# Three sums of each up product: from VectorE and POOL to accumulating transfers between SBUF tiles

## The chip, the cores and the metric

One core of a Trainium2 chip runs the kernel. Its engines work side by side and each takes its own instructions in order: TensorE (PE in the profile) multiplies matrices into PSUM, VectorE (DVE) and ScalarE (ACT) read PSUM and SBUF, GpSimd (POOL) reads SBUF, SyncE (SP) here only begins transfers, and 16 DMA engines carry them out. An engine waits for another, or for a transfer, by semaphores. The metric is the device time of one execution in microseconds.

## The reference

Two blocks follow one another. The first is a linear attention without softmax, on 8 batches, 8 heads, 576 positions and 64 features, with an RMS norm. Its output, as 4608 rows of 512, goes through four experts; each row adds up the four results by its own weights.

```python
kv = einsum('bhsd,bhse->bhde', k, v)
out = einsum('bhsd,bhde->bhse', q, kv)
x = out / sqrt(mean(out * out, -1) + 1e-6) * g_norm      # then (b, s, h*d): 4608 x 512
p = domain_probs / (domain_probs.sum(-1) + 1e-9)
for e in range(4):
    h = maximum(x @ w1[e], 0)                            # "up": 512 -> 1024
    y += p[:, e:e+1] * (h @ w2[e])                       # "down": 1024 -> 512
```

All of it is float32, and the experts' products are nearly all of the work.

## The kernel before

The rows are cut into 9 blocks of 512, so there are 36 steps `s = e * 9 + c` (expert `e`, block `c`). In each step an up product and, one step behind, a down product run interleaved on TensorE. Each product is done by a seven-product scheme of Strassen's kind, in two levels: 7 outer products `m`, each made of 7 inner products `mm`. The blocks of the result are sums and differences of the outer products. It is these outer sums that the change is about.

The program does not give its instructions in the order in which they run. Every operation goes into a plan with a key (where in the steps it belongs), a cost on each engine that may take it, and its buffers. The plan then plays the program through by these costs and fixes for each engine which operation it takes and when, and in which buffer each value lies. That order is the one the chip runs.

```python
def layout(self, slots, later, idle, idle_banks, idle_until):
    ...                                   # (cut: choice of the operation with the nearest due time)
    if eng == "SP":
        ...
    else:
        op.end = busy[eng] = t + op.cost[eng]
        if op.kb:                         # a transfer begun on an engine other than SP
            op.end += 5.5
    if op.port:
        port = op.end                     # one "combine" at a time on VectorE or POOL
```

Costs of an operation on `n` elements a partition, and the helper that all elementwise sums in SBUF go through (line 360 of the profile):

```python
def dve(n):    return {"DVE": 0.155 + 0.00104 * n}
def act(n):    return {"ACT": 0.155 + 0.00088 * n}
def either(n): return {"DVE": 0.155 + 0.00104 * n, "POOL": 0.15 + 0.00225 * n}

def combine(key, cost, out_, a, b, op, reads, writes):
    plan.add(key, cost,
        lambda eng: adder(eng).tensor_tensor(out=out_(), in0=a(), in1=b(), op=op),
        reads=reads, writes=writes, port=True)
```

The up product of a step. Each outer product `m` is collected in a tile `made[m]` of 128 x 1024 (kind `big`, 29 tiles and later 4 more). ScalarE copies (line 900) and VectorE sums (line 908) bring it out of PSUM, and both free the PSUM bank for TensorE:

```python
OUTER = (1, 2, 6, 5, 3, 7, 4)
def up(s, e, views):
    made, h = {}, {}

    def add(key, to, a, b, op=ALU.add, where=either):
        combine(key, where(2 * NT), lambda: to.ap[:], lambda: a.ap[:], lambda: b.ap[:], op, [a, b], [to])

    def relu(key, b):                     # line 864, ScalarE, 128 x 1024
        ...

    for i, m in enumerate(OUTER):
        whole = made[m] = Buf("big", f"m{n}")
        ...                               # (cut: 7 inner products on TensorE, L881, with their copies and sums)
        key = s + (i + 1) / 7

        def unit(f):
            h[f] = Buf("big", f"h{f}_{s}")
            return h[f]

        if m == 2:
            add(key, unit(1), made[1], made[2])
            relu(key, h[1])
        elif m == 6:
            add(key, made[1], made[1], made[6])
        elif m == 5:
            add(key, made[6], made[1], made[5])
        elif m == 3:
            add(key, unit(21), made[6], made[3])
            relu(key, h[21])
            add(key, unit(7), h[1], h[21], ALU.subtract)
        elif m == 7:
            add(key, made[1], made[1], made[7])
            add(key, unit(4), made[1], made[5], where=dve)
            relu(key, h[4])
            ...                           # (cut: two more sums on VectorE)
        elif m == 4:
            add(key, unit(2), made[1], made[4])
            relu(key, h[2])
            add(key, unit(3), h[2], h[6], ALU.subtract)
```

The down product of the later experts begins its four groups with 0.2 of a step's offset, `h[1]` and `h[6]` first and `h[2]` in the third. Its results are added to the output in HBM by transfers begun on POOL (line 1065), 256 KB each:

```python
def send(key, i):
    ...
    nc.gpsimd.dma_start(out=dst, in_=cell(i)[parts, :], accum_op=ALU.add)   # e > 0; else a plain one on SP
```

Steps 9 to 35 have the inner scheme in the down product too (line 1170 on TensorE); the first expert's down product (line 1095) has one level, with matmuls of 256 columns. The forms of x for each step come from HBM by transfers begun on SP, one 512 KB form or two halves for each `m`.

Of the kernel before, what the change touches and what calls it, by code (L numbers as in the profile page):

```python
# [10 lines left out]
ALU = mybir.AluOpType  # L11
# [219 lines left out]
def kernel(  # L231
# [36 lines left out]
    nc = tc.nc  # L268
# [65 lines left out]
    plan = Plan()  # L334

    def pe(products, columns, passes=2):
        return {"PE": passes * products * (0.008 + 0.0008125 * columns) + 0.003}

    def dve(n):
        return {"DVE": 0.155 + 0.00104 * n}  # L340

    def act(n):
        return {"ACT": 0.155 + 0.00088 * n}
# [12 lines left out]
    def combine(key, cost, out_, a, b, op, reads, writes):  # L356

        plan.add(
            key, cost,
            lambda eng: adder(eng).tensor_tensor(out=out_(), in0=a(), in1=b(), op=op),  # L360
            reads=reads, writes=writes, port=True,
        )
# [485 lines left out]
    def block(b, a, t):  # L848
        return b.ap[:, (2 * a + t) * HN:(2 * a + t + 1) * HN]

    def up(s, e, views):
        made = {}
        h = {}

        def add(key, to, a, b, op=ALU.add, where=either):
            combine(
                key, where(2 * NT), lambda: to.ap[:], lambda: a.ap[:], lambda: b.ap[:], op,
                [a, b], [to],
            )

        def relu(key, b):
            plan.add(
                key, act(2 * NT),
                lambda eng: nc.scalar.activation(out=b.ap[:], in_=b.ap[:], func=ACT.Relu),  # L864
                reads=[b], writes=[b],
            )

        for i, m in enumerate(OUTER):
            n = f"{s}_{m}"
            whole = made[m] = Buf("big", f"m{n}")  # L870
            bank = {
                1: Buf("u1", f"u1_{n}"), 2: Buf("u2", f"u2_{n}"), 5: Buf("u2", f"u3_{n}"),
            }
            snap = {}
            for j, mm in enumerate(ORDER):
                key = s + (i + j / 7) / 7
                ps = bank[{2: 2, 5: 5, 3: 5}.get(mm, 1)]

                def product(eng, m=m, mm=mm, ps=ps):
                    for u in range(2):  # L880
                        nc.tensor.matmul(  # L881
                            ps.ap[:, u * P:(u + 1) * P],
                            lhsT=w1f[e][m][mm][1]()[:, u * P:(u + 1) * P], rhs=views[m][mm][1](),
                            start=(mm in (1, 5) and u == 0), stop=True, skip_group_check=True,
                        )

                op = plan.add(
                    key, pe(2, P), product,
                    reads=w1f[e][m][mm][0] + [views[m][mm][0]] + ([ps] if mm == 2 else []),
                    **{"parts" if mm == 2 else "writes": [ps]},  # L890
                    after=last[-2:-1] if mm == 1 else seeds if mm == 5 else (),
                )
                op.marks, op.seed = (ps, HN), mm == 2
                if mm == 3:
                    last.append(op)

                def copy(to, where, ps=ps, key=key):
                    return plan.add(
                        key - 0.4, act(HN),
                        lambda eng: nc.scalar.activation(  # L900
                            out=where(), in_=ps.ap[:, 0:HN], func=ACT.Copy),
                        reads=[ps], parts=[to],
                    )

                def total(a, t, src, add_, whole=whole, key=key):
                    plan.add(
                        key - 0.4, dve(HN),
                        lambda eng: nc.vector.tensor_tensor(  # L908
                            out=block(whole, a, t), in0=src.ap[:, 0:HN], in1=add_.ap[:], op=ALU.add),
                        reads=[src, add_], parts=[whole],  # L910
                    )

                if mm == 1:
                    seeds = [copy(bank[2], lambda b=bank[2]: b.ap[:, 0:HN])]
                elif mm in (6, 7):
                    snap[mm] = Buf("snap", f"s{mm}_{n}")
                    copy(snap[mm], lambda b=snap[mm]: b.ap[:])
                if mm == 2:
                    copy(whole, lambda whole=whole: block(whole, 0, 0))
                elif mm == 7:  # L920
                    total(1, 1, bank[5], snap[7])
                elif mm == 4:
                    copy(whole, lambda whole=whole: block(whole, 1, 0))
                elif mm == 3:
                    total(0, 1, ps, snap[6])
            key = s + (i + 1) / 7

            def unit(f):
                h[f] = Buf("big", f"h{f}_{s}")
                return h[f]  # L930

            if m == 2:
                add(key, unit(1), made[1], made[2])
                relu(key, h[1])
            elif m == 6:
                add(key, made[1], made[1], made[6])
            elif m == 5:
                add(key, made[6], made[1], made[5])
            elif m == 3:
                add(key, unit(21), made[6], made[3])  # L940
# [6 lines that stand above are left out]
                add(key, unit(5), h[21], h[4], where=dve)  # L947
                add(key, unit(6), h[5], h[1], ALU.subtract, dve)
            elif m == 4:
                add(key, unit(2), made[1], made[4])  # L950
                relu(key, h[2])
                add(key, unit(3), h[2], h[6], ALU.subtract)
        hidden[s] = h
# [333 lines left out]
    for e in range(E):  # L1287
        for c in range(NCH):
            s = e * NCH + c
# [10 lines left out]
            if s:  # L1300
                up(s, e, x_views.pop(s))
# [25 lines left out]
    with tc.manual_schedule(engines={ENG.PE, ENG.DVE, ENG.Activation, ENG.Pool, ENG.SP}):  # L1327
# [4 lines left out]
        for op in order:  # L1332
# [6 lines left out]
            made = op.fn(op.eng)  # L1339
# [34 lines left out]
```

## Time and profile before

| what | value |
|---|---|
| time, median of 3 | 1731.64 us (1731.56 to 1731.66) |
| span of the profiled execution | 1729.4 us, granted TensorE clock 0.999 |
| sums of 128x1024 on VectorE, out of `big` into `big` | 263, mean 1330 ns |
| the same on POOL | 43, mean 2363 ns |
| sums of 128x512 on POOL, `big<-big` | 52, mean 1281 ns |
| sums of 128x256 out of PSUM on VectorE, L908 | 430, mean 422 ns |
| ReLU on ScalarE, L864, 128x1024 | 128, mean 1051 ns |
| copies on ScalarE, L900, 128x256 | mean 371 to 383 ns |
| issues of transfers on POOL, L1065 | 112; 256 KB, at block 8 of an expert 128 KB |

Read it so. "Busy" is the time in which an engine ran instructions. The chain of waits is followed back from the last instruction of the program, at each step to what released it, and tells which engine set the end. A group of instructions has a line, an engine, an operation and a tile, with the idle time before it and what ended that. The landing of a transfer is counted from its issue to the semaphore that tells of its last byte. What is idle on an engine off the chain costs nothing.

### The profile page before, as it was taken

Reading aid. Unit: us, or ns where it says so; the run is one execution under the profiler, and the core shown is the slowest. Engines: PE = TensorE matmul, PEld = TensorE weight load, DVE = VectorE, ACT = ScalarE, POOL = GpSimd, SP = SyncE. Lnnn points to the kernel's source line nnn. Section 1 sums busy time; section 2 is a strip of 40 time slices with the busy share of each in tenths; the row PEclk is TensorE's granted clock in tenths of the full one; section 3 lists DMA queues with packets and bytes.
Section 4 is the critical chain, followed back from the end, with each engine's and each line's share of the span. In section 5 each row is a group of like instructions: output and inputs, shape, how many; then the busy total and the mean of one; then the engine's idle time right before and its main releaser. Section 6 shows DMA issues by size and latency. Waiting matters only on the chain.

```text
span 1729.4 us, 38448 instructions
## 1 busy us (share of the span) xinstructions
PE 1719.6 (99%) x15334; PEld 1652.0 (96%) x15334; DVE 1222.8 (71%) x1968; ACT 938.6 (54%) x2300; POOL 616.5 (36%) x561
## 2 busy tenths in 40 slices
PE   9999999999999999999999999999999999999998
PEld 7699999999999999999999999999999999999997
DVE  4755655565676777777788877777788877777774
ACT  3354544454444565656555556566555556665652
POOL 3421323133334333333345333333345333333331
PEclk9999999999999999999999999999999999999999
DMA  9756444633333343534465344444475344444442
GB/s 240 218 161 193 153 122 131 193 135 128 147 130 99 94 114 104 116 106 113 131 185 110 99 110 111 111 111 110 114 204 110 98 111 111 110 110 109 112 99 49
DMA packets 148596, 220.94 MB, mean 128 GB/s; under 512 B 49600, under 2 KB 90816, under 8 KB 148416
## 3 DMA queue, kind: packets, MB, share of 16 engines
q1 hardware_dynamic: 133312, 191.21, 35.6%
q0 software_dynamic: 15104, 27.27, 11.0%
q8 instruction: 120, 1.97, 0.5%
q14 instruction: 60, 0.49, 0.1%
HBM read 145.30 MB, written 73.14 MB: 126 GB/s over the span
## 4 chain that ended last, share of the span: by engine, by line
PE 99%; POOL 0%; ACT 0%; DVE 0%; issue 0%; POOLq 0%
PE u L881 45%; PE db L1170 19%; PE db L1095 15%; PE ab L1170 12%; PE ab L1095 2%; PE u L968 2%; PE ab L634 1%; PE ab L678 1%; PE ab L620 1%; PE ab L1323 1%; PE ab L660 1%; PE db L660 0%; POOL rt L551 0%; PE ab L722 0%; PE ab L704 0%; PE ab L738 0%
## 5 line engine op out<-in xcount | busy, mean ns | idle before, releaser
L360 DVE TENSOR_TENSOR big<-big,big 128x1024 f32<-128x1024 f32 (+1 forms) x449 | 440.9, 995 | 34.9 <-ACT big L864 23.8
L881 PE MATMUL u<-xf,big 128*128 128x128 f32 x3104 | 453.3, 276 | 0.0
L881 PEld LDWEIGHTS u<-xf,big 128*128 128x128 f32 x3104 | 401.5, 192 | 2.2
L881 PE MATMUL u<-xf,w1y 128*128 128x128 f32 x2652 | 389.9, 276 | 0.0
L908 DVE TENSOR_TENSOR big<-u,snap 128x256 f32<-128x256 f32 x430 | 181.3, 422 | 235.9 <-PE u L881 176.4
L881 PEld LDWEIGHTS u<-xf,w1y 128*128 128x128 f32 x2652 | 343.6, 192 | 2.1
L900 ACT ACTIVATE snap<-u 128x256 f32<-128x256 f32 x490 | 187.7, 383 | 251.6 <-PE u L881 212.2
L1095 PE MATMUL db<-big,big 128*128 128x256 f32 x1136 | 269.0, 382 | 2.1 <-DVE big L560 2.1
L1095 PEld LDWEIGHTS db<-big,big 128*128 128x128 f32 x1136 | 207.1, 192 | 25.4 <-DVE big L560 2.3
L900 ACT ACTIVATE big<-u 128x256 f32<-128x256 f32 x430 | 164.7, 383 | 110.6 <-PE u L881 75.5
L360 POOL TENSOR_TENSOR big<-big,big 128x256 f32<-128x256 f32 (+1 forms) x139 | 172.5, 1248 | 132.3 <-DVE big L360 46.8
L1170 PE MATMUL db<-big,big 128*128 128x128 f32 x1056 | 146.9, 276 | 0.4 <-ACT snap L1198 0.4
L864 ACT ACTIVATE big<-big 128x1024 f32<-128x1024 f32 x128 | 134.5, 1051 | 3.4 <-POOL big L360 2.1
L1170 PEld LDWEIGHTS db<-big,big 128*128 128x128 f32 x1056 | 132.1, 192 | 0.6 <-ACT snap L1198 0.6
L1236 POOL TENSOR_TENSOR big<-big 128x512 f32<-128x512 f32 x26 | 33.0, 1268 | 269.2 <-DVE big L360 263.9
L1198 ACT ACTIVATE snap<-db 128x256 f32<-128x256 f32 x192 | 68.4, 356 | 100.0 <-PE db L1170 95.1
L360 POOL TENSOR_TENSOR big<-big 128x512 f32<-128x512 f32 (+1 forms) x57 | 70.3, 1232 | 126.8 <-DVE big L360 102.6
L1170 PE MATMUL db<-kv,big 128*128 128x128 f32 x804 | 114.7, 275 | 0.0
L1065 POOL DMA_DIRECT2D out_dram<-big x100 | 91.2, 987 | 47.4 <-ACT snap L1198 22.8
L900 ACT ACTIVATE u<-u 128x256 f32<-128x256 f32 x245 | 90.9, 371 | 28.1 <-PE u L881 8.0
L1170 PEld LDWEIGHTS db<-kv,big 128*128 128x128 f32 x804 | 102.1, 192 | 0.1
L1206 DVE TENSOR_TENSOR big<-ab,snap 128x256 f32<-128x256 f32 x140 | 59.1, 422 | 57.4 <-ACT snap L1198 31.9
(213 smaller groups left out, 2676.9 us busy)
## 6 DMA issues: line engine op xcount, KB each, us to landing
xf<-x SPq DMA_DIRECT2D x108, 512.0 KB, 3.6
out_dram<-big POOLq DMA_DIRECT2D x84, 256.0 KB, 5.8
xf<-x_h SPq DMA_DIRECT2D x81, 256.0 KB, 3.2
xf<-x SPq DMA_DIRECT2D x81, 256.0 KB, 3.3
x<-xf SPq DMA_DIRECT2D x36, 512.0 KB, 6.1
big<-in_moe_w_dram SPq DMA_DIRECT2D x25, 512.0 KB, 4.8
small<-in_q_dram SPq DMA_DIRECT2D x72, 128.0 KB, 4.8
kv<-in_k_dram SPq DMA_DIRECT2D x30, 288.0 KB, 4.8
```

The source lines that it names most:

```text
L360: lambda eng: adder(eng).tensor_tensor(out=out_(), in0=a(), in1=b(), op=op),
L864: lambda eng: nc.scalar.activation(out=b.ap[:], in_=b.ap[:], func=ACT.Relu),
L881: nc.tensor.matmul(ps.ap[:, u * P:(u + 1) * P], lhsT=w1f[e][m][mm][1]()[:, u * P:(u + 1) * P], rhs=views[m][mm][1](), start=(mm in (1, 5) ...
L900: lambda eng: nc.scalar.activation(out=where(), in_=ps.ap[:, 0:HN], func=ACT.Copy),
L908: lambda eng: nc.vector.tensor_tensor(out=block(whole, a, t), in0=src.ap[:, 0:HN], in1=add_.ap[:], op=ALU.add),
L968: nc.tensor.matmul(bank.ap[:], lhsT=two(w.ap[:])[:, kt, ut * P:(ut + 1) * P], rhs=two(xh[dh].ap[:])[:, kt, :], start=(dh == kt == 0), stop ...
L1065: nc.gpsimd.dma_start(out=dst, in_=cell(i)[parts, :], accum_op=ALU.add)
L1095: nc.tensor.matmul(ps.ap[:, 0:HN], lhsT=four(h[m])[:, kt // 2, t, kt % 2, :], rhs=w2f[e][m].ap[:, kt * HN:(kt + 1) * HN], start=(m in (1, ...
L1170: nc.tensor.matmul(ps.ap[:, o * P:(o + 1) * P], lhsT=b.ap[:, col:col + P], rhs=w2q[e][m][mm][1]()[:, kt, :], start=(mm in (1, 5) and o == ...
L1198: lambda eng: nc.scalar.activation(out=where(), in_=group_of(ps.ap), func=ACT.Copy),
L1206: lambda eng: nc.vector.tensor_tensor(out=cell(tq, dq), in0=group_of(src.ap), in1=group_of(add_.ap), op=ALU.add,),
L1236: lambda eng: adder(eng).tensor_tensor(out=whole(to), in0=whole(a), in1=whole(b), op=ALU.add),
```

## The change

In steps 9 to 33 three of the sums of each up product are no longer instructions of VectorE or POOL. A transfer adds one SBUF tile to another on its way: `made[2] += made[1]`, `made[6] += made[1]` and `made[4] += made[1]`. It is begun on POOL, like the accumulating transfers to the output. The result then lies in the tile that was the second summand, so the tiles change their names: `h[1]` is what was `made[2]`, `h[2]` what was `made[4]`, and the sum of 1 and 6 goes on in `made[6]`, for which a new tile is taken at `m == 5`. The purpose is to take elementwise work off VectorE and POOL, and the port to SBUF that these two share. The plan counts 1.0 us on POOL for such a transfer, and lets it end 5.5 us after that by the line shown above.

```diff
+        by_dma = e > 0 and s < 34
+
+        def accumulate(key, to, a):
+
+            plan.add(
+                key, {"POOL": 1.0},
+                lambda eng: nc.gpsimd.dma_start(out=to.ap[:], in_=a.ap[:], accum_op=ALU.add),
+                reads=[a, to], writes=[to], kb=512,
+            )
+
...
-            if m == 2:
+            if m == 2 and by_dma:
+                h[1] = made[2]
+                accumulate(key, h[1], made[1])
+                relu(key, h[1])
+            elif m == 2:
                 add(key, unit(1), made[1], made[2])
                 relu(key, h[1])
+            elif m == 6 and by_dma:
+                accumulate(key, made[6], made[1])
+                made[1] = made[6]
+                made[6] = None
             elif m == 6:
                 add(key, made[1], made[1], made[6])
             elif m == 5:
+                made[6] = made[6] or Buf("big", f"v{s}")
                 add(key, made[6], made[1], made[5])
...
             elif m == 4:
-                add(key, unit(2), made[1], made[4])
+                if by_dma:
+                    h[2] = made[4]
+                    accumulate(key, h[2], made[1])
+                else:
+                    add(key, unit(2), made[1], made[4])
                 relu(key, h[2])
                 add(key, unit(3), h[2], h[6], ALU.subtract)
```

The matmuls stay as they are. As the plan is played through anew, the order of the instructions changes on every engine from step 9 on, and with it which sums VectorE takes and which POOL.

## The prediction

> **What bounds the kernel now.** I read four views. First the page's busy times and the chain of waits that ended last, to see which engine sets the end. Then a table of stretches of 100 us, to see whether that engine has anything left in the part that the change touches. Then who waited for whom on TensorE, and last the transfers.
>
> ```profile
> PE 1719.6 (99%) x15334; PEld 1652.0 (96%) x15334; DVE 1222.8 (71%) x1968; ACT 938.6 (54%) x2300; POOL 616.5 (36%) x561
> ...
> PE 99%; POOL 0%; ACT 0%; DVE 0%; issue 0%; POOLq 0%
> ```
>
> The chain is TensorE from one end to the other; VectorE, which the change relieves, is in it with 0%. But matmul ends are modelled, so "100% busy" need not mean full speed. The stretches settle that (columns: PE, PEld, DVE, ACT and POOL busy us with the number of records, granted clock, DMA share, GB/s):
>
> ```profile
> 600.00:700.00 100.00, 100.00 (x898) 100.00 (x897) 77.40 (x118) 62.18 (x159) 39.24 (x36) 1.00 0.48 111
> 700.00:800.00 100.00, 100.00 (x898) 100.00 (x897) 74.56 (x117) 59.62 (x150) 35.16 (x33) 1.00 0.45 113
> ...
> 1500.00:1600.00 100.00, 100.00 (x898) 100.00 (x897) 73.50 (x115) 59.85 (x150) 31.98 (x30) 1.00 0.42 106
> ```
>
> A float32 matmul leaves two records. 100 us over 898 records is 111.4 ns a record, 222.7 ns a matmul of 128 columns, the same in every stretch without first-expert work, and the loads of the weights show no gap either. The waits listed for TensorE sum to 5.4 us of 1729 in six lines, these the longest:
>
> ```profile
> PE db L1095 <- DVE big L560: 2.1, 1, 2.1
> PE ab L1323 <- POOL ident masks.py:199: 1.4, 1, 1.4
> PE u L881 <- ACT snap L900: 0.6, 1, 0.6
> PE u L881 <- ACT u L900: 0.5, 1, 0.5
> ```
>
> So nothing waits that VectorE could release. What a faster VectorE can give back between about 440 and 1690 us is under 1 us.
>
> The second set of lines is for the price of a transfer: the issues on POOL (form, shortest, median and longest ns of the issue), their time to landing, and the page's queue lines.
>
> ```profile
> L1065 POOL DMA_DIRECT2D out_dram<-big x100: 804/920/1224, 603.0 to 1703.5; - x100
> ...
> DMA to landing us min/median/max: 3.1/5.7/9.4
> ```
>
> ```profile
> q1 hardware_dynamic: 133312, 191.21, 35.6%
> q0 software_dynamic: 15104, 27.27, 11.0%
> ```
>
> **What the Trainium skill says.** "TensorE: Matmul & The Clock Gate", section "Wait — 56ns, not 53.3ns?", gives N/2.4 GHz plus about 2.5 ns from start to start, 55.6 ns at 128 columns. If each record is two such passes, that is 111.2 ns as an estimate; the trace has 111.4. TensorE is therefore at its own limit here, and no freed engine makes it faster. "DMA: Bandwidth & Descriptors", section "Anatomy of one DMA — SWDGE (gpsimd) path", fits 2.0 us plus bytes over 436 GB/s, which would be 2.6 us for the 256 KB transfers begun on POOL. The trace has a median of 5.7, so I use the trace. The same page, section "SWDGE vs HWDGE vs iDMA", says accumulation exists only on the path begun by GpSimd: POOL must issue, in order, with its 0.92 us. "SBUF — State Buffer", section "Who interferes with whom", says that a VectorE instruction with two SBUF inputs contends with a GpSimd one that reads SBUF. The trace agrees: beside a POOL sum of 2.64 us a VectorE sum of 256 elements took 2.31 us.
>
> ```profile
> 691.86 2.64 POOL L360 TENSOR_TENSOR big<-big,small 128x1024 f32<-128x1024 f32 x1
> ...
> 692.49 2.31 DVE L360 TENSOR_TENSOR big<-big,big 128x256 f32<-128x256 f32 x1
> ```
>
> **The change part by part.** Steps 9 to 33 are touched, 25 steps of three sums: 75 sums of 128x1024 go, 75 transfers of 512 KB come.
>
> 1. VectorE and POOL. In the order of the built instructions VectorE loses 74 of the 75 sums and POOL one. The layout then moves 22 sums of 512 and 10 of 256 elements from POOL to VectorE. VectorE: 74 x 1.33 us (the row of 128x1024 sums) is 98 us less, and 22 x 0.9 + 10 x 0.5 is 25 us more, so about 1150 us busy instead of 1223. POOL: 2.4 + 22 x 1.28 + 10 x 0.75 = 38 us less, 75 x 0.92 = 69 us more. Both lie beside TensorE: worth 0.
>
> 2. Matmuls. Their number and shapes are the same, 7884 in both. Worth 0.
>
> 3. DMA engines. q0 took 0.110 x 16 x 1729.4 = 3044 us of engine time for 27.27 MB, 112 us per MB. q1 took 9850 us for 191.21 MB, 51.5 us per MB. An accumulating byte costs 2.2 times a plain one. 512 KB is 0.524 MB, so 58.5 engine-us, or 3.7 us on each of 16 engines. 75 of them are 275 us on each engine over the 1290 us concerned: the share rises from about 0.45 to about 0.65. The engines aren't filled, but loads and transfers will lengthen one another.
>
> 4. The latency, the only part that can touch the end. A 256 KB transfer lands after 5.7 us (median) and its data take half of 3.7, so a 512 KB one should land 5.7 + 1.8 = 7.5 us after its issue, with a spread like that of the old ones: 4.9 to 11. A sum on VectorE took 1.33 us. The sum is thus some 6 us later for whoever needs it.
>
> 5. Who needs it. Two of the three sums of a step are followed by a ReLU on ScalarE, which is an in-order queue that also carries the PSUM copies that TensorE waits for. If the transfer lands late, the ReLU holds the copies up, and the copies hold TensorE up. I counted the matmuls in TensorE's order between the last one that the sum depends on and the first one that depends on the ReLU or on what stands behind it on ScalarE. That is 47 to 53 in nearly all steps (47 and 53, or 49 and 51, for the two ReLUs). 47 x 0.2224 = 10.5 us. Off go the ReLU (1.05) and the copy behind it (0.38) and about 0.2 for semaphores: the data must be there 8.6 to 8.8 us after the matmul. The issue starts about 1.0 us after it (0.2 of wait, the 0.42 us VectorE sum out of PSUM, POOL's queue). So the transfer has 7.6 us in the tightest place (one sum in every second step, 12 places) and 8.0 to 8.5 in the other 38. The third sum goes to an add; 69 to 83 matmuls lie before its deadline, more than 11 us for the transfer. It is free.
>
> 6. The tightest place has two output transfers of 256 KB just ahead of it in POOL's queue, whose data (1.8 us each) go first. At the two later changes of expert only 29 to 41 matmuls lie between, some of them 256 columns wide (about 0.43 us each): 8 to 9 us.
>
> Sum: with a median of 7.5 and a spread of about 1.2 us against 7.6, a tight place overruns by 0.4 to 0.5 us on average: 12 x 0.45 = 5 us. Against 8.2 the mean overrun is about 0.15: 38 x 0.15 = 6 us. Changes of expert: 2 us. Less what a destination in SBUF may save against one in HBM, which no row shows; I take 4 us off. About +9 us: **1740 us**.
>
> **The rivals.**
> - The latency is hidden altogether. For: the kernel's own plan puts 1.0 + 5.5 us on each of these transfers, near the landing seen, and orders ScalarE by it. Short old transfers landed in 3.1. Then the time is 1731 to 1733. Against: the plan lets transfers of POOL overlap freely, without the bytes in front of them.
> - The transfers are much slower than their bytes say, say 10 us, because two SBUF sides and the x loads (512 KB each, seven forms a step) share the engines. Each ReLU then overruns by 1.5 to 2.5 us and TensorE takes it over nearly whole: 50 x 2 = 100 us, 1830 us. For: the old landings go up to 9.4. Against: a DMA share of 0.45 leaves room.
> - The freed VectorE shortens the path. For: it is 75% busy in these stretches and its 2.31 us sum shows a collision. Against: the 898 records per 100 us. At most 1 us, 1731.
> - The x loads come late because the engines are shared. They land after 3.3 to 3.6 us and no matmul waits for one, so I give this next to nothing.
>
> **Range and chances.** Nothing can bring 2%: 0.01. 2% slower is 34.6 us, which is 0.7 us on each of 50 ReLUs; that needs a landing about 1.3 us over my 7.5, well within what I don't know: 0.18. The rest, 0.81, is within 2%. The range is 1731 to 1768: hidden altogether at one end, 0.7 us a ReLU at the other.
>
> **What would show it.** Right: TensorE waits at the lines of the up and down products released by ScalarE copies, 5 to 15 us more than before; ScalarE waits for DMA at the ReLU line; landings with a median near 7.5 us; VectorE near 1150 us busy; q0 near 3044 + 75 x 58.5 = 7430 us of engine time, a share of 27% of 16 engines; fewer than 898 records in 100 us, in the stretches from step 9 on only. Wrong: landings of 5 us and no waits (time unchanged), landings of 9 us and more with ReLU waits of 1 us and more in each step (the second rival), or waits of TensorE for loads of x.

## The result and the profile after

The changed kernel takes 1753.13 us (1749.97 to 1755.1, four runs) against 1731.6 us: a ratio of 1.0123, 95% interval 1.0106 to 1.0141. It is 21.5 us slower. The prediction had the direction and the engine, but about 9 us.

The page's busy times and chain of waits:

```profile
PE 1728.1 (99%) x15334; PEld 1654.1 (94%) x15334; DVE 1131.6 (65%) x1926; ACT 934.3 (53%) x2300; POOL 645.2 (37%) x603
...
PE 88%; DMA 7%; POOL 2%; ACT 1%; DVE 1%; issue 1%; POOLq 0%; ACTq 0%; DVEq 0%
```

VectorE lost 91 us of work, and the time rose. Transfers, which were not in the chain at all, now make 7% of it. TensorE has the same 15334 records. The span is 22.9 us longer; 14.4 of that is idle time of TensorE (span less busy, 24.2 us against 9.8), and 8.5 us is more "busy" time for the same matmuls, which stand further apart (the last section says why the profile counts this as busy). The stretches (columns as before) show where:

```profile
600.00:700.00 100.00, 98.83 (x880) 98.31 (x880) 67.32 (x112) 61.25 (x157) 42.22 (x42) 1.00 0.64 146
700.00:800.00 100.00, 99.15 (x883) 98.60 (x881) 61.97 (x105) 57.40 (x145) 39.38 (x39) 1.00 0.66 149
...
1100.00:1200.00 100.00, 97.02 (x864) 96.44 (x863) 64.59 (x109) 58.41 (x148) 40.32 (x41) 1.00 0.61 138
...
1500.00:1600.00 100.00, 99.06 (x884) 98.67 (x883) 66.93 (x113) 60.81 (x155) 42.47 (x42) 1.00 0.64 144
```

Where there were 898 records in 100 us there are 864 to 884 in these four. At 111.4 ns each, the 34 that are missing from 1100 to 1200 are 3.8 us. The loss is spread over most of the changed steps; the stretch from 900 to 1000 us has none (792 records against 794). Who waited for whom, first on TensorE, then on ScalarE (total us, times, longest us):

```profile
PE u L891 <- ACT snap L910: 13.8, 16, 1.8
```

```profile
ACT big L874 <- DMA big<-big: 34.1, 20, 3.4
...
ACT big L874 <- DMA big<-small: 8.2, 3, 3.1
```

L874 is the ReLU. It waits 23 times for a transfer, 42.3 us in all. Before (there it is L864) it never did, and its longest waits in total were these, for sums:

```profile
ACT big L864 <- POOL big L360: 2.1, 3, 1.3
ACT big L864 <- DVE big L360: 1.2, 3, 0.5
```

TensorE now waits for PSUM copies (L910) of ScalarE. The issues and landings of the 75 new transfers (L867; the line shows 52 of them, the other 23 differ in the kind of tile), the landing of the output transfers (L1088), and the queues:

```profile
L867 POOL DMA_DIRECT2D big<-big x52: 860/880/1182, 521.6 to 1634.4; - x52
...
DMA to landing us min/median/max: 4.5/7.4/11.0
```

```profile
DMA to landing us min/median/max: 3.3/6.5/10.9
```

```profile
q1 hardware_dynamic: 133312, 191.21, 35.4%
q0 software_dynamic: 25904, 66.60, 21.9%
```

The median, 7.4 us, is the 7.5 that was predicted. But it is the median of three quite different kinds. Sorted by which sum of the step each one carries (25 of each, read from the trace issue by issue):

| sum | what stands just ahead in POOL's queue | landing us, least / median / most |
|---|---|---|
| h2 (m = 4) | mostly nothing | 4.6 / 5.4 / 8.4 |
| h1 (m = 2) | two output transfers or more in 21 steps, nothing in 4 | 4.5 / 8.9 / 11.0 |
| 1 and 6 (m = 6) | the h1 transfer | 5.8 / 7.4 / 8.8 |

21 of the ReLU's 23 waits are for an h1 transfer: for the 21 that have output transfers ahead of them, which land after 8.1 to 11.0 us. The other four land after 4.5 to 5.2 us, and no ReLU waits for them. One of the 21 in the chain that ended last, in order of time (start us, us, what):

```profile
1196.13 0.86 POOL out_dram L1088
...
1197.11 9.19 DMA big<-big
...
1206.32 1.06 ACT big L874
...
1207.41 0.69 DVE big L360
1208.10 0.34 DVE big L918
...
1208.49 1.16 PE u L891 x8
```

The output transfer is issued, then the h1 transfer, which lands after 9.2 us. The ReLU starts 20 ns after that, a sum of VectorE starts behind the ReLU, and behind it in VectorE's order stands the sum out of PSUM that TensorE needs. The timelines of the same place show, on ScalarE, the copies that piled up behind the ReLU and, on TensorE, what waited for the first of them (the last bracket is idle time and what ended it):

```profile
1203.54 0.37 ACT L1221 ACTIVATE ab<-db 128x256 f32<-128x256 f32 x1 [0.45 <-PE db L1193]
1206.32 1.06 ACT L874 ACTIVATE big<-big 128x1024 f32<-128x1024 f32 x1 [2.42 <-DMA big<-big]
1207.28 0.37 ACT L910 ACTIVATE snap<-u 128x256 f32<-128x256 f32 x1
1207.55 0.38 ACT L910 ACTIVATE u<-u 128x256 f32<-128x256 f32 x1
1207.85 0.38 ACT L1221 ACTIVATE snap<-db 128x256 f32<-128x256 f32 x1
```

```profile
1207.70 0.71 PE L891 MATMUL u<-xf,big 128*128 128x128 f32 x4 [1.07 <-ACT snap L910]
```

After an idle 2.4 us ScalarE runs without a pause: the copies behind the ReLU had been ready. TensorE was idle for 1.07 us, until the first of them was done. So a wait of the ReLU reaches TensorE only in part: the ReLUs waited 42.3 us, and the time rose by 21.5.

### The profile page after: what moved, and what is told of

It is laid out like the page before. It is cut to its first block, busy times and chain, and to the rows that moved or that the text cites. A ratio compares the mean times of both kernels' runs of the same rounds, so it can differ in the third digit from the quotient of the medians.

```text
span 1752.3 us, 38626 instructions
## 1 busy us (share of the span) xinstructions
PE 1728.1 (99%) x15334; PEld 1654.1 (94%) x15334; DVE 1131.6 (65%) x1926; ACT 934.3 (53%) x2300; POOL 645.2 (37%) x603
## 4 chain that ended last, share of the span: by engine, by line
PE 88%; DMA 7%; POOL 2%; ACT 1%; DVE 1%; issue 1%; POOLq 0%; ACTq 0%; DVEq 0%
PE u L891 39%; PE db L1193 16%; PE db L1118 14%; PE ab L1193 10%; DMA big<-big 5%; PE ab L1118 2%; DMA big<-small 2%; PE u L991 2%; PE ab L634 1%; POOL out_dram L1088 1%; PE ab L678 1%; PE ab L620 1%; PE ab L1346 1%; PE ab L660 1%; DVE big L360 1%
## 5 line engine op out<-in xcount | busy, mean ns | idle before, releaser
L891 PE MATMUL u<-xf,big 128*128 128x128 f32 x3392 | 491.2, 276 | 13.3 <-ACT snap L910 13.3
L891 PEld LDWEIGHTS u<-xf,big 128*128 128x128 f32 x3392 | 436.0, 192 | 19.4 <-ACT snap L910 16.6
L360 DVE TENSOR_TENSOR big<-big,big 128x1024 f32<-128x1024 f32 (+1 forms) x391 | 380.1, 980 | 48.7 <-ACT big L874 28.9
L918 DVE TENSOR_TENSOR big<-u,snap 128x256 f32<-128x256 f32 x446 | 187.9, 421 | 240.9 <-PE u L891 182.3
L910 ACT ACTIVATE snap<-u 128x256 f32<-128x256 f32 x490 | 187.7, 383 | 234.1 <-PE u L891 178.7
L360 POOL TENSOR_TENSOR big<-big,big 128x256 f32<-128x256 f32 (+1 forms) x145 | 193.4, 1336 | 219.8 <-DVE big L360 114.2
L910 ACT ACTIVATE big<-u 128x256 f32<-128x256 f32 x446 | 170.7, 383 | 120.4 <-PE u L891 81.5
L1118 PEld LDWEIGHTS db<-big,big 128*128 128x128 f32 x1128 | 205.0, 191 | 25.2 <-DVE big L560 2.3
L874 ACT ACTIVATE big<-big 128x1024 f32<-128x1024 f32 x130 | 136.8, 1052 | 46.0 <-DMA big<-big 34.1
L1193 PE MATMUL db<-big,big 128*128 128x128 f32 x960 | 134.8, 275 | 0.4 <-ACT snap L1221 0.4
L360 DVE TENSOR_TENSOR big<-big 128x512 f32<-128x512 f32 (+1 forms) x111 | 88.7, 801 | 56.4 <-ACT big L874 55.1
L1193 PEld LDWEIGHTS db<-big,big 128*128 128x128 f32 x960 | 120.7, 192 | 0.6 <-ACT snap L1221 0.6
L360 POOL TENSOR_TENSOR big<-big 128x512 f32<-128x512 f32 (+1 forms) x47 | 60.0, 1277 | 123.6 <-DVE big L360 100.6
L910 ACT ACTIVATE u<-u 128x256 f32<-128x256 f32 x245 | 91.2, 372 | 23.9 <-PE u L891 4.9
L1088 POOL DMA_DIRECT2D out_dram<-big x98 | 90.2, 1049 | 23.3 <-ACT big L1065 8.7
```

The lines of the kernel that those rows point to most:

```text
L891: nc.tensor.matmul(ps.ap[:, u * P:(u + 1) * P], lhsT=w1f[e][m][mm][1]()[:, u * P:(u + 1) * P], rhs=views[m][mm][1](), start=(mm in (1, 5) ...
L910: lambda eng: nc.scalar.activation(out=where(), in_=ps.ap[:, 0:HN], func=ACT.Copy),
L918: lambda eng: nc.vector.tensor_tensor(out=block(whole, a, t), in0=src.ap[:, 0:HN], in1=add_.ap[:], op=ALU.add),
L1118: nc.tensor.matmul(ps.ap[:, 0:HN], lhsT=four(h[m])[:, kt // 2, t, kt % 2, :], rhs=w2f[e][m].ap[:, kt * HN:(kt + 1) * HN], start=(m in (1, ...
L1193: nc.tensor.matmul(ps.ap[:, o * P:(o + 1) * P], lhsT=b.ap[:, col:col + P], rhs=w2q[e][m][mm][1]()[:, kt, :], start=(mm in (1, 5) and o == ...
```

## The experiments

**Theory 1.** The h1 transfer waits in POOL's queue behind two output transfers of 256 KB. It lands later than the plan believed when it placed the ReLU on ScalarE. ScalarE, in order, holds up the copies that TensorE needs. **Theory 2.** The 75 transfers crowd the DMA engines by their bytes, whatever the order. **Theory 3.** The new order of the instructions costs the time, not the transfers. All times beside 1731.3 us of the kernel before; the changed kernel's ratio is to the 1731.6 above.

| run | us | ratio, 95% interval | h1 / m = 6 / h2 landing, median us | ReLU's waits for a transfer, us |
|---|---|---|---|---|
| changed kernel | 1753.1 | 1.0123 (1.0106 to 1.0141) | 8.9 / 7.4 / 5.4 | 43.4 |
| e1_first_only | 1747.0 | 1.0091 (1.0076 to 1.0106) | 8.4 / - / - | 25.0 |
| e2_last_only | 1734.2 | 1.0019 (1.0011 to 1.0028) | - / - / 5.4 | 0 |
| e3_middle_only | 1731.9 | 1.0004 (0.9995 to 1.0013) | - / 5.9 / - | 0 |
| e8_without_first | 1734.4 | 1.0018 (1.0012 to 1.0025) | 5.4, both together | 0.7 |
| e5_short_sums | 1731.7 | 1.0003 (0.9995 to 1.0012) | 6.6 / 4.5 / 2.7 | 0 |
| e6_short_outputs | 1732.2 | 1.0006 (0.9998 to 1.0015) | 5.4 / 6.0 / 5.1 | 1.3 |
| e10_half_outputs | 1731.5 | 1.0000 (0.9992 to 1.0009) | 6.4 / 6.0 / 5.1 | 2.3 |
| e7_outputs_behind | 1732.0 | 1.0004 (0.9995 to 1.0013) | 5.3 / 6.1 / 5.2 | 0 |
| e4_plan_longer | 1734.1 | 1.0017 (1.0010 to 1.0024) | 7.2 / 6.0 / 5.6 | 0 |
| e9_plan_first | 1732.1 | 1.0004 (0.9995 to 1.0013) | 8.8 / 6.9 / 5.3 | 0.7 |

The landings by sum are read from the trace issue by issue. The changed kernel's 43.4 adds 1.1 us at a ReLU on another kind of tile to the 42.3 above.

**Which of the three sums.** Each kernel switches one or two of the three transfers back to sums on VectorE or POOL, for example e1:

```diff
-            elif m == 6 and by_dma:
+            elif m == 6 and False:
...
-                if by_dma:
+                if False:
```

> Only the sum for h1 (m = 2) is a transfer, 25 in all; the other two stay sums on VectorE or POOL. Theory 1 (the transfer for h1 stands behind two output transfers in POOL's queue, lands after 8.5 to 11 us, and the ReLU that waits for it holds up the PSUM copies on ScalarE): nearly the whole loss stays, 1746 to 1753 us, with ScalarE waiting for DMA at the ReLU for 30 to 45 us in all. Theory 2 (the transfers' total bytes crowd the DMA engines): a third of the loss, about 1739. Theory 3 (the new order of instructions, not the transfers, costs the time): anything; no wait of ScalarE for DMA is needed.

> Only the sum for h2 (m = 4) is a transfer, 25 in all, which in the changed kernel was issued ahead of the output transfers and landed after 4.5 to 6 us. Theory 1: the loss is gone but for the two changes of expert, 1731 to 1734 us; ScalarE waits for DMA at the ReLU for under 4 us in all. Theory 2: a third of the loss, about 1739. Theory 3: anything.

> Only the sum of 1 and 6 (m = 6) is a transfer, 25 in all. An add, not a ReLU, waits for it, on POOL or VectorE. Theory 1: no wait on ScalarE, 1731 to 1733 us. Theory 2: a third of the loss, about 1739.

> The sums for h2 (m = 4) and of 1 and 6 (m = 6) are transfers, 50 in all; the one for h1 stays a sum on VectorE or POOL. Theory 1: two thirds of the bytes but hardly any of the loss, 1731 to 1736 us. Theory 2: two thirds of the loss, about 1746.

The h1 transfers alone cost 15.7 us with a third of the bytes; the other two sums together, with two thirds of the bytes, cost 3.1. That speaks against theory 2. The ReLU's waits in e1 were 25 us, fewer than I expected. A likely reason can be read from the traces, though no run tests it: in the changed kernel the ReLU of h1 stands 32 matmuls behind the last one that its sum depends on in about every second step and 38 in most others, with waits of 1.8 to 2.6 us at most of the former and 0.8 to 1.4 at most of the latter; in e1 it is 38 in nearly all. The other 6 us of the loss come only when all three are transfers; they are not separated further.

The 15.7 us are not all waiting either. The two longest waits of TensorE in e1, 2.27 and 2.44 us, were each followed by 3.4 us at half the granted clock, which the changed kernel does not have after any of its waits for the ReLU's copies. That makes about 3.4 of the 15.7 us (an estimate: 2 x 3.4 us x 1/2), and leaves about 12 for the waits.

e2 and e8 are 3 us over the kernel before with hardly a wait at the ReLU (0 and 0.7 us). In both, and in e1, TensorE waits 1.2 us for VectorE at the down product with 256 columns, where it did not before; the rest of these 3 us is open. These waits lie in the last step; steps 17, 26 and 35, block 8 of each later expert, have the one-level down product too, which the section on the kernel before leaves out. Here for e8 (total us, times, longest us):

```profile
PE db L1118 <- DVE big L1072: 0.6, 1, 0.6
PE ab L1118 <- DVE big L1072: 0.6, 1, 0.6
```

**The bytes, in an unchanged order.** These three keep the changed kernel's instructions in their order on every engine; only the width of the transfers differs. e5 leaves out the last 960 of 1024 columns of each of the 75 sums, e6 the last 448 of 512 columns of the later experts' results, e10 the last 256 of them.

```diff
-                lambda eng: nc.gpsimd.dma_start(out=to.ap[:], in_=a.ap[:], accum_op=ALU.add),
+                lambda eng: nc.gpsimd.dma_start(out=to.ap[:, 0:64], in_=a.ap[:, 0:64], accum_op=ALU.add),
...
-                        nc.gpsimd.dma_start(out=dst, in_=cell(i)[parts, :], accum_op=ALU.add)
+                        nc.gpsimd.dma_start(out=dst[:, 0:64], in_=cell(i)[parts, 0:64], accum_op=ALU.add)
```

> The changed kernel, with every one of the 75 transfers moving only the first 64 of 1024 columns (the rest of each sum is left out). Instructions and their order on every engine are those of the changed kernel. Theories 1 and 2: the h1 transfers still stand behind the output transfers, but their own data take 0.3 us and not 2.7, so they land 2 to 3 us earlier, at 5.5 to 7 us; the waits of ScalarE go and the time falls to 1731 to 1734. Theory 3: it stays at about 1753.

> The changed kernel, with the output transfers begun on POOL moving only the first 64 of 512 columns (the rest of the results of the later experts is left out). Instructions and their order are those of the changed kernel, and the 75 transfers are whole. Theory 1: with nothing long in front of them the h1 transfers land after 5 to 6 us, ScalarE doesn't wait, 1731 to 1734 us. Theory 2 (their own bytes, and the loads beside them): the 75 transfers keep most of their latency and the time stays above 1745. Theory 3: about 1753.

> The changed kernel in its own order, with the output transfers begun on POOL moving 256 of 512 columns (the other half of the later experts' results is left out). Theory 1: half as much stands in front, so the h1 transfers land about halfway between 5.4 us (64 columns) and 8.9 us (all), at 7 to 7.5. That is just under the 7.6 to 8.5 us that I counted as harmless, so 1732 to 1737 us and waits of ScalarE at the ReLU of 3 to 15 us. Were the count wrong by a microsecond (harm from 6.5 us on), it would be 1741 to 1745.

Theory 3 falls: with the same order the loss is gone in all three. e6 and e10 separate the other two: there the 75 transfers are whole, and only what stands ahead of them is shorter. The h1 landing falls from 8.9 to 6.4 us with half outputs and to 5.4 with short ones, and the loss is gone in both. Taking bytes out of the outputs also takes load off the DMA engines, so these two alone would not settle it against theory 2; the next does. e10 landed a little earlier than I expected (6.4, not 7 to 7.5), and its largest h1 landing, 7.3 us, did no harm: the count of 7.6 us as a limit is not contradicted, and a limit of 6.5 is. The delay is not in proportion to the bytes ahead: whole outputs cost 3.5 us, half outputs 1.0.

e5 has a second reading. VectorE and POOL are free of the sums there, no ReLU waits for a transfer (one copy does, for 0.8 us), and TensorE waits at the up product as before:

```profile
PE u L891 <- ACT snap L910: 0.6, 1, 0.6
PE u L891 <- ACT u L910: 0.5, 1, 0.5
```

It runs in 1731.7 us. That is what the freed work is worth here: nothing that these runs can measure.

**What stands ahead.** All transfers whole, but the second pair of output transfers of a step is made to depend on the h1 transfer in the plan. In POOL's queue it then comes behind the h1 and the m = 6 transfer.

```diff
+                first = accumulate(key, h[1], made[1])
+                for o in held_back.pop(s - 2, ()):
+                    o.deps[first] = True
...
+                held_back[s] = [send(key, 0), send(key, 1)]
```

> The changed kernel with all 75 transfers whole and all output transfers whole, but the second pair of output transfers of a step may be issued only when the h1 transfer has ended by the plan, so that the pair stands behind the h1 and the m = 6 transfer in POOL's queue, not ahead. Theory 1 (what stands ahead in the queue is the cause): h1 lands after 5 to 6.5 us, ScalarE's waits for DMA at the ReLU fall from 43 us to under 8, and the time is 1731 to 1735 us. Theory 2 (bytes crowd the engines, whatever the order): the bytes are the same, the time stays at 1747 to 1754.

The bytes are those of the changed kernel, the DMA share is the same, and the loss is gone. h1 lands after 5.3 us. The stretch from 1100 to 1200 us of this kernel beside that of the changed one:

```profile
1100.00:1200.00 100.00, 100.00 (x898) 100.00 (x897) 65.17 (x105) 59.40 (x150) 37.36 (x39) 1.00 0.63 151
```

DMA share 0.63 (0.61 in the changed kernel), and 898 records again. The plan was played through anew, so other instructions moved as well, but not the ReLU of h1: in most steps it stands 36 matmuls behind, as in the changed kernel (32 to 38). Theory 2 falls.

**The place of the ReLU.** In e4 the plan is told that each of these transfers ends 9.5 us after its issue (`op.end += 9.5 if op.kb == 512 else 5.5`), in e9 that the h1 transfer alone ends 10 us after it. The edit of e9:

```diff
-                            op.end += 5.5
+                            op.end += op.late if hasattr(op, 'late') else 5.5
...
-                accumulate(key, h[1], made[1])
+                accumulate(key, h[1], made[1]).late = 10.0
```

> The changed kernel, but the plan lets a 512 KB transfer begun on POOL end 9.5 us after its issue and not 5.5, so that it sets the ReLU later in ScalarE's order, behind the PSUM copies that TensorE needs first. The transfers, their bytes and what stands ahead of them in the queue stay nearly as they were. Theory 1 with the step that I call the harm (the late ReLU in ScalarE's in-order queue, not the late data as such): the h1 transfers still land after 8 to 11 us, but ScalarE waits for them under 8 us in all and the time is 1731 to 1735. If late data harm TensorE in another way (buffers, the later sums), it stays above 1742.

> The changed kernel, but the plan lets the h1 transfer alone end 10 us after its issue; the other two keep 5.5. The h1 transfer still stands behind two output transfers in POOL's queue; its ReLU stands some 58 matmuls after the matmul that the sum waits for, not 32 to 38. If the harm is the ReLU's place in ScalarE's in-order queue: h1 still lands after 8 to 11 us, ScalarE waits for DMA at the ReLU for under 5 us in all, 1731 to 1735 us. If late data harm TensorE in another way: above 1742.

e9 is the sharpest of the runs. The h1 transfers still stand behind the outputs and still land after 8.8 us, and it takes 1732.1 us. No transfer was made faster; the ReLU stands later in ScalarE's order, where in most steps 58 matmuls and not 32 to 38 lie between. (Here too the new plan moved other instructions.) The ReLU's waits for transfers, in all:

```profile
ACT big L874 <- DMA big<-big: 0.7, 1, 0.7
```

So the late data as such did no harm here, only the instructions held behind them. In e4 the h1 transfers landed earlier (7.2 us), since its plan moved the transfers too. It has 2.8 us left, 1.7 of them in waits of TensorE for VectorE's sums out of PSUM.

No version beats the kernel before: e3, e5, e6, e7, e9 and e10 can't be told from it, and TensorE leaves nothing to win.

## Why the prediction was right or wrong

1. VectorE and POOL, right. VectorE 1132 us busy (1150 predicted), POOL 645 (647 by its sum). Worth nothing: shown by e5.
2. Matmuls, right: the same 15334 records, no gain anywhere.
3. DMA engines, the size wrong. The share of about 0.65 came (0.58 to 0.70). But q0 took 0.219 x 16 x 1752.3 = 6140 us of engine time, not 7430: if the outputs cost what they did before, a new transfer costs (6140 - 3044) / 75 = 41 engine-us, 2.6 us on each engine and not 3.7.
4. The latency, wrong as a single figure. The median came out as predicted, 7.4 against 7.5, but by luck, as two errors cancel: a transfer with nothing ahead lands after 5.4 us, one behind two outputs after 8.9.
5. Who needs it, the mechanism right: the ReLU in ScalarE's in-order queue holds the copies. Part of it goes on through VectorE, which I did not list: the chain shows the sum of VectorE that waits for the ReLU, ahead of its sum out of PSUM. The limit of 7.6 to 8.5 us stands, and the changed kernel's own trace gives it: in eight steps of one kind, with h1 landing after 8.5 to 9.3 us, the landing less the idle time of TensorE that follows it (0.4 to 1.2 us) is 8.1 us each time. That overrun then reaches TensorE, as predicted.
6. **The step that failed.** "The tightest place has two output transfers of 256 KB just ahead of it in POOL's queue, whose data (1.8 us each) go first." I saw this and left it out of the sum, which still used a landing of 7.5 us with a spread of 1.2, and twelve places: "12 x 0.45 = 5 us". Behind the outputs the landing was 8.9, and not in 12 steps but in nearly all: in the other steps the outputs belong further ahead by the matmuls they wait for, yet POOL issued them right before the h1 transfer too. 21 of 25 ReLUs of h1 waited, 0.8 to 3.4 us each. By the prediction's own terms the 25 places of h1 make 5 us for the twelve tight ones and 13 x 0.15 = 2 us for the rest; measured they cost 15.7 (e1), some 12 of them as waits. The other 25 of the 38 places are h2's, for which its terms make 25 x 0.15 = 4 us; h2 and m = 6 together cost 3.1, with no wait at the ReLU but 0.7 us. And the 4 us were taken off in the wrong place: transfers with nothing ahead did land earlier than I said (5.4, not 7.5), but those of h1, which cost the time, did not.

Of the rivals, the hidden latency is what h2 and m = 6 nearly show. The slow transfer of 10 us is what h1 comes close to, for one sum of a step and not for two, and because of what stood ahead, not because of two SBUF sides; and TensorE took over about half of the ReLUs' waits, not nearly all. The freed VectorE gave nothing. No matmul waited for a load of x.

## What to carry to other kernels

A transfer's latency is that of its place in the queue: look at what is issued just ahead on the same queue, here two transfers of 256 KB that put 3.5 us on top of 5.4, and never take one median for all. When an engine works in order, count what stands behind the reader of a late operand; here that, and not the late operand itself, cost the time. So either move the long transfers behind the urgent one (e7) or move the reader back (e9). And before taking work off an engine, see whether that engine is in the chain: 91 us less on VectorE brought nothing, because TensorE ran at 111.4 ns a record, in the changed steps almost without a gap.

## What the runs showed of the hardware

Packets of the transfers that add one SBUF tile to another took about twice as long as plain ones of the same size: the trace has 328 ns (median) for 4096 bytes of the new transfers and 159 for plain ones, and 178 against 84 at 2048 bytes with a destination in HBM. The plain ones are begun on SP and the adding ones on POOL; no run has a plain transfer begun on POOL, so whether the adding or the queue makes the difference is not shown. Per byte, the adding packets into SBUF took 0.080 ns against 0.087 into HBM at the median, and 0.083 against 0.102 in the mean (341 and 209 ns a packet). They also differ in size, so how much of this is the destination's is open.

The idle time that the profile lists for TensorE is less than a stall costs. A matmul's record lasts about 275 ns and the next one starts 111 ns after it, so the first 0.16 us of every wait count as busy. That is part of why of the 22.9 us of the longer span only 14.4 are idle and 8.5 are counted as busy.

A long wait of TensorE was followed by a lower clock. In e1, after its waits of 2.27 and 2.44 us, the granted clock was 0.5 for 3.4 us, and four matmul records took 1.22 us where they had taken 0.61:

```profile
883.63 0.61 PE L1193 MATMUL db<-kv,big 128*128 128x128 f32 x4
886.50 1.22 PE L891 MATMUL u<-xf,big 128*128 128x128 f32 x4 [2.27 <-ACT snap L910]
```

The wait of 2.1 us near 73 us was followed by the same 3.4 us in the traces of the kernel before and the changed one, while the changed kernel's longest wait behind a ReLU, 1.84 us, was not.
